# Linear attention in a fused kernel: token outputs from one head's 64 rows at a time, a one-step remainder, and half the transposes

## The chip, the cores and the metric

The kernel runs on one core of one Trainium2 chip. The metric is the device time in microseconds (us) of one execution. Three timed runs of the kernel before gave 1415.54, 1417.77 and 1420.30 us; their median, 1417.77 us, is the time before. The profile comes from one further execution.

## The reference

```python
kv  = einsum('bhsd,bhse->bhde', k, v)          # 8 batches, 8 heads, 576 tokens, 64 x 64 per head
out = einsum('bhsd,bhde->bhse', q, kv)
x   = out / sqrt(mean(out * out, -1) + 1e-6) * g_norm     # then as 4608 tokens x 512
xn, en = x / |x|, expert_emb / |expert_emb|               # 8 experts
logits = xn @ en.T / tau                                  # each token goes to its best expert
y   = gate * (relu(x @ w1[e]) @ w2[e])                    # e: the token's expert
h   = y @ w_in
result = (h * cos(h)) @ w_out
```

Everything is float32. The change touches the first two lines and the numerators of the logits; the experts and the last two matrices are computed as before.

## The kernel before

The program has three stages that follow one another: attention with the routing of the tokens, the experts (`layer1`, `layer2`), and the last layer (`step`, `out_product`). Only the first is touched.

It walks 36 tiles of 128 tokens. Nine tiles make a round over two batches: four tiles of 128 tokens of each batch, and as the ninth the last 64 tokens of both. For a tile `t` the loop at L869 issues in this order:

- `emit_out(t)` (L672): for each of four head pairs a matmul over all 128 rows. The left side holds two heads' transposed queries on 64 rows each, the right side is `kvb`, a 128 x 144 block: the two heads' 64 x 64 matrices on its diagonal, zeros beside them, and 16 columns for the two heads' products with the 8 expert vectors. The ninth tile of a round takes 64 tokens from each of two batches, so there each matmul fills 64 columns of the array, and two of them stand side by side. The result is the PSUM tile `po`, of which there are three.
- `emit_square(t)` and `emit_root(t-1)` on ScalarE; `emit_qT(t+2)` (L660): four transposes of queries into PSUM and a copy on ScalarE.
- what the table `due` (L845) names for this tile: `kv_pair`, the sum over tokens for two heads of a coming batch (four steps over 128 tokens each, and the remainder of 64 tokens as two steps on 32 rows); `"t"`, `kv_transpose`: four 128 x 128 transposes of `kvb`; `"z"`, `kv_logits`: four matmuls of 128 x 16 that make the 16 columns.
- the counting matmuls for the routing (L778, L779), in every third tile, which write to unused columns of `po`.
- `emit_x(t)` (L698) on VectorE: the norm's root, then two reads of `po` of the tile before, scaled (`z`, `xg`). After the `xg` of a tile its `po` is free for a later `emit_out`. Between these, `advance` takes steps of `place(g)`: three tiles at a time, VectorE picks the expert, GpSimd counts, and GpSimd scatters the rows to DRAM with three indirect DMAs.

Each engine works in the order of issue. GpSimd's queue holds, for each group of three tiles, the cast `pi`, three scatters (L789), and the product `w` of the next group (L757), for which VectorE waits in L761. The token loads of all batches go out through SP's queue, three batches ahead. In the second part of the stage ScalarE and VectorE also split weights for the experts (`split_piece`).

When a batch's sums are done (`kv_pair` with `hp == 3`), ScalarE copies the two diagonal blocks into `kvb` with two copies of 64 partitions. The zeros around them were set once, at the start, by GpSimd. A float32 matmul is recorded as two matmuls and two weight loads, so four of them are eight records; a transpose is recorded once.

Of the kernel before, what the change touches and what calls it, by code (L numbers as in the profile page):

```python
# [21 lines left out]
DM = H * D  # L22
# [3 lines left out]
NTILE = NT // 128  # L26
KVW = 128 + 2 * E
XZ = DM + E
# [8 lines left out]
def tile_kernel(ctx, tc, q, k, v, g_norm, emb, tau, w1, w2, w_in, w_out, out):  # L37
# [435 lines left out]
    if True:  # L473
# [18 lines left out]

        kr, vr = (kp.tile([128, H, 2, D], F32, name=nm, tag=nm, bufs=1) for nm in ("kr", "vr"))

# [95 lines left out]
        def prepare_experts():  # L590
            nc.scalar.activation(out=en, in_=embt, func=ACTF.Square, accum_out=es[:, 0:1])
            nc.vector.tensor_scalar(out=es[:, 1:2], in0=es[:, 0:1], scalar1=1e-30, scalar2=None, op0=ALU.max)
            nc.scalar.activation(out=es[:, 2:3], in_=es[:, 1:2], func=ACTF.Ln)
            nc.scalar.activation(out=es[:, 3:4], in_=es[:, 2:3], func=ACTF.Exp, scale=-0.5)
            for _ in rsqrt_steps(es[:, 3:4], es[:, 1:2], 0.0, 1.0, es[:, 3:4], es[:, 4:5]):
                pass
            nc.vector.tensor_tensor(out=es[:, 5:6], in0=es[:, 0:1], in1=es[:, 3:4], op=ALU.mult)
            nc.vector.scalar_tensor_tensor(
                out=es[:, 5:6], in0=es[:, 5:6], scalar=1e-6, in1=taub, op0=ALU.add, op1=ALU.mult
            )  # L600
            nc.vector.reciprocal(out=es[:, 6:7], in_=es[:, 5:6])
            nc.vector.tensor_scalar(out=en, in0=embt, scalar1=es[:, 6:7], scalar2=None, op0=ALU.mult)
            pe = ps_t.tile([128, 4, 128], F32, name="qTp", tag="qTp")
            for hp in range(4):
                nc.tensor.transpose(out=pe[:, hp, 0:E], in_=en[:, hp * 128:(hp + 1) * 128], identity=ident[0:E, 0:E])
            for i in range(2):
                r = slice(64 * i, 64 * i + 64)
                nc.vector.tensor_scalar(out=gz[r, :, i, :], in0=pe[r, :, 0:E], scalar1=g2[r], scalar2=None, op0=ALU.mult)

# [3 lines left out]
        def kv_pair(b, hp):  # L613
            if hp == 0:
                kvp_t[b] = ps_s.tile([128, 4, 128], F32, name="kvp", tag="kvp")
            p, dst = kvp_t[b], kvb[b % 3]
            rr = slice(32 * (b % 4), 32 * (b % 4) + 32)
# [12 lines left out]
        kvs_t = {}  # L630

        def kv_transpose(b):
            dst = kvb[b % 3]
            p = ps_s.tile([128, 4, 128], F32, name="kvp", tag="kvp")
            for hp in range(4):
                nc.tensor.transpose(out=p[:, hp, :], in_=dst[:, hp, 0:128], identity=ident)
            kvs_t[b] = tp.tile([128, 4, 128], F32, name="kvs", tag="kvs")
            nc.scalar.activation(out=kvs_t[b], in_=p, func=ACTF.Copy)

        def kv_logits(b):  # L640
            a = kvs_t.pop(b)
            p = ps_s.tile([128, 4, 128], F32, name="kvp", tag="kvp").rearrange("p c x -> p (c x)")
            for hp in range(4):
# [4 lines left out]
            nc.scalar.activation(  # L648
                out=kvb[b % 3][:, :, 128:KVW], in_=p[:, 0:8 * E].rearrange("p (c x) -> p c x", c=4), func=ACTF.Copy
            )  # L650
# [19 lines left out]
        ms_t, po_t = {}, {}  # L670

        def emit_out(t, po):  # L672
# [12 lines left out]
        def emit_square(t):  # L685
            sq = tp.tile([128, H, D], F32, name="sq", tag="sq")
            nc.scalar.activation(out=sq.rearrange("p (c n) d -> p c (n d)", c=4), in_=po_t[t][:, :, 0:128], func=ACTF.Square)
            ms_t[t] = sq
# [9 lines left out]
        def emit_x(t):  # L698
# [15 lines left out]
            advance(1)  # L714
            po = po_t.pop(t - 1)
            yb = y.rearrange("p (c n o) -> p c n o", c=4, o=1)
# [4 lines left out]
            nc.vector.tensor_tensor(  # L721
                out=z.rearrange("p (c n) x -> p c n x", c=4), in0=po[:, :, 128:KVW].rearrange("p c (n x) -> p c n x", n=2),
                in1=yb.to_broadcast([128, 4, 2, E]),
                op=ALU.mult,
            )
            advance(1)
            nc.vector.tensor_tensor(
                out=xg[g][:, i, 0:DM].rearrange("p (c n d) -> p c n d", c=4, n=2),
                in0=po[:, :, 0:128].rearrange("p c (n d) -> p c n d", n=2), in1=yb.to_broadcast([128, 4, 2, D]), op=ALU.mult,
            )  # L730
# [11 lines left out]
        def place(g):  # L742
# [32 lines left out]
            yield RANK  # L775
            c0 = KVW + g % 4 * E * n
            prv = cur["po"][:, 0, c0:c0 + E * n]
# [91 lines left out]
        for t in range(NTILE):  # L869
# [526 lines left out]
```

## Time and profile before

| | us |
|---|---|
| median of three runs | 1417.77 |
| the profiled execution | 1422.97 |
| its span, first to last instruction | 1421.4 |
| TensorE busy in the span | 1355.4 |
| VectorE busy | 1017.4 |
| ScalarE busy | 843.2 |
| GpSimd busy | 234.7 |
| first and last token-output matmul (start) | 25.9 and 140.8 |

The token outputs, `kv_pair`, transposes and logits all lie in the first tenth of the span; the rest belongs to the experts and the last layer. A chain of waits is read backwards from the last instruction: at each step it names what released the instruction, or the instruction before it on its engine, so the TensorE pieces in it are the spacing of starts, without the pipeline's tail. In groups of instructions the mean duration does include that tail.

### The profile page before, as it was taken

The page shows a single profiled execution, that of the slowest core. Times are in us where ns is not written, and L with a number is a line of the kernel's source. Part 1 is how long each engine was busy: PE and PEld are TensorE (multiplying, and loading weights), DVE is VectorE, ACT ScalarE, POOL GpSimd, SP SyncE. Part 2 cuts the span into 40 slices and gives each one's busy share as a digit, 9 for nine tenths or more (in the row PEclk, how much of TensorE's full clock was granted, in tenths as well). Part 3 has the DMA queues.
Part 4 walks back from the last instruction along what each step waited for, and adds up shares of the span by engine and source line. Part 5 has one row for each costly group of instructions (what it writes and reads, how often), then busy time and mean ns, then how long its engine had stood idle before and what let it go on. Part 6 is the DMA issues. An engine that isn't in the chain of part 4 may idle for free.

```text
span 1421.4 us, 26588 instructions
## 1 busy us (share of the span) xinstructions
PE 1355.4 (95%) x9545; PEld 1256.0 (88%) x9545; DVE 1017.4 (72%) x2179; ACT 843.2 (59%) x1647; POOL 234.7 (17%) x281
## 2 busy tenths in 40 slices
PE   8997799999999999998899999999999999999995
PEld 8886799899999999987789889889889889889894
DVE  1668688798888888566677677676776767777662
ACT  3668344464555454346676777677666767667662
POOL 0244442232422334100010010101001010010101
PEclk8999899999999999999999999999999999999998
DMA  9997386878987786385575655746656565655630
GB/s 293 337 336 217 123 216 173 263 237 236 232 246 226 203 247 169 90 279 192 170 236 178 216 193 171 249 159 212 210 186 210 183 215 182 211 188 185 206 105 32
DMA packets 210212, 291.74 MB, mean 205 GB/s; under 512 B 23468, under 2 KB 117200, under 8 KB 208856
## 3 DMA queue, kind: packets, MB, share of 16 engines
q1 hardware_dynamic: 191112, 243.25, 55.6%
q0 software_dynamic: 7296, 29.45, 6.5%
q10 hardware_dynamic: 11664, 17.26, 4.0%
q8 instruction: 78, 1.28, 0.4%
q14 instruction: 62, 0.51, 0.1%
HBM read 241.42 MB, written 48.47 MB: 204 GB/s over the span
## 4 chain that ended last, share of the span: by engine, by line
PE 81%; DVE 7%; DMA 4%; ACT 3%; issue 2%; POOL 0%; SPq 0%; ACTq 0%; DVEq 0%; POOLq 0%
PE o L1206 27%; PE p L1113 24%; PE hps L233 12%; PE y L250 12%; PE po L677 2%; PE kvp L621 1%; DMA raw<-in_moe_w 1%; PE xp L216 1%; DVE ring L141 1%; PE qTp L665 1%; PE kvp L624 1%; DMA ws<-wa 1%; DVE ring L344 1%; ACT ring L343 1%; DMA xr<-xs 0%
## 5 line engine op out<-in xcount | busy, mean ns | idle before, releaser
L1206 PE MATMUL o<-ring,g 128*128 128x512 f32 x1728 | 415.1, 395 | 2.3 <-ACT ring L343 1.6
L1206 PEld LDWEIGHTS o<-ring,g 128*128 128x128 f32 x1728 | 319.7, 188 | 75.5 <-issue 1.8
L233 PE MATMUL hps<-xT,ring 128*128 128x304 f32 x1536 | 244.6, 309 | 8.1 <-DVE xT L222 6.2
L250 PE MATMUL y<-h,ring 128*128 128x304 f32 x1536 | 238.1, 304 | 4.3 <-issue 2.7
L233 PEld LDWEIGHTS hps<-xT,ring 128*128 128x128 f32 x1536 | 222.5, 191 | 9.7 <-DVE xT L222 6.9
L250 PEld LDWEIGHTS y<-h,ring 128*128 128x128 f32 x1536 | 222.1, 189 | 5.8 <-issue 3.6
L1138 DVE TENSOR_TENSOR r<-u,h 128x512 f32<-128x512 f32 x144 | 99.7, 693 | 104.8 <-ACT u L1137 101.2
L1218 POOL DMA_INDIRECT out<-o_sb,perm_i x36 | 39.4, 1095 | 792.8 <-ACT o_sb L1217 621.1
L1094 ACT ACTIVATE u<-h 128x512 f32<-128x512 f32 x144 | 89.9, 624 | 96.8 <-DVE h L1129 95.8
L239 ACT ACTIVATE h<-hps 128x304 fp32r<-128x304 f32 x128 | 53.5, 418 | 116.8 <-PE hps L233 115.5
L1133 ACT ACTIVATE r<-u 128x512 f32<-128x512 f32 x144 | 89.8, 623 | 53.7 <-DVE u L1098 53.7
L1095 ACT ACTIVATE r<-h 128x512 f32<-128x512 f32 x144 | 89.8, 624 | 45.2 <-DVE g L1147 45.2
L1113 PEld LDWEIGHTS p<-ring,wb 128*128 128x128 f32 x840 | 106.3, 194 | 6.7 <-DVE h L1129 5.3
L1113 PE MATMUL p<-ring,wb 128*128 128x256 f32 x840 | 107.2, 288 | 4.4 <-DVE h L1129 4.4
L1113 PEld LDWEIGHTS p<-ring,wa 128*128 128x128 f32 x840 | 104.7, 191 | 5.7 <-DVE h L1129 2.9
L1113 PE MATMUL p<-ring,wa 128*128 128x256 f32 x840 | 106.1, 286 | 3.3 <-DVE h L1129 2.3
L1137 ACT ACTIVATE u<-r,half_pi 128x512 f32<-128x512 f32 x144 | 104.2, 724 | 4.7
L174 POOL TENSOR_TENSOR gx<-xr,g_bc 76x512 f32<-76x512 f32 x64 | 105.4, 1674 | 3.1 <-ACT gx L183 3.1
L1098 DVE SCALAR_TENSOR_TENSOR u<-r,u 128x512 f32<-128x512 f32 x144 | 95.7, 688 | 13.4 <-ACT r L1095 10.7
L141 DVE TENSOR_TENSOR ring<-raw,ring 128x1024 fp32r<-128x1024 f32 x72 | 92.3, 1283 | 11.7 <-ACT ring L140 11.0
L1147 DVE TENSOR_TENSOR g<-r,g 128x512 fp32r<-128x512 f32 x144 | 92.8, 686 | 0.2 <-ACT g L1143 0.2
L240 DVE SCALAR_TENSOR_TENSOR h<-hps,h 128x304 fp32r<-128x304 f32 x128 | 59.5, 465 | 36.5 <-ACT h L239 31.4
(219 smaller groups left out, 1908.9 us busy)
## 6 DMA issues: line engine op xcount, KB each, us to landing
wa<-ws SPq DMA_DIRECT2D x252, 256.0 KB
wb<-ws SPq DMA_DIRECT2D x252, 256.0 KB
raw<-in_moe_w SPq DMA_DIRECT2D x144, 256.0 KB
ws<-wa SPq DMA_DIRECT2D x56, 256.0 KB
xr<-xs POOLq DMA_DIRECT2D x16, 627.0 KB
yT<-yo SPq DMA_DIRECT2D x64, 152.0 KB
km<-in_k SPq DMA_DIRECT2D x8, 1024.0 KB
vm<-in_v SPq DMA_DIRECT2D x8, 1024.0 KB
```

The costliest lines, as they stand in the source:

```text
L141: nc.vector.tensor_tensor(out=w[:, 1], in0=raw, in1=w[:, 0].bitcast(F32), op=ALU.subtract)
L174: nc.gpsimd.tensor_tensor(out=gx[:, r].rearrange("p (h d) -> p h d", h=H), in0=t[:, r, 0:DM].rearrange("p (h d) -> p h d", h=H), in1=g_bc[ ...
L233: nc.tensor.matmul(out=p[:, 0:CH], lhsT=w[:, a, k * 128:(k + 1) * 128], rhs=c["xT"][b_][k], start=(n == 0), stop=(n == 11),)
L250: nc.tensor.matmul(out=c["y"][d][:, 0:CH], lhsT=w[:, a, 512 + d * 128:512 + (d + 1) * 128], rhs=h[b_], start=(f == 0 and i == 0), stop=(f ...
L1094: nc.scalar.activation(out=u, in_=p, func=ACTF.Copy, scale=1.0 / (2 * math.pi))
L1095: nc.scalar.activation(out=r, in_=p, func=ACTF.Copy, scale=1.0 / (2 * math.pi), bias=ROUND)
L1098: V.scalar_tensor_tensor(out=u, in0=r, scalar=-ROUND, in1=u, op0=ALU.add, op1=ALU.subtract)
L1113: nc.tensor.matmul(out=out, lhsT=w[:, wi, a, k * 128:(k + 1) * 128], rhs=x[xi][:, b_, k * 256:(k + 1) * 256], start=(n == 0), stop=(n == 5),)
L1137: nc.scalar.activation(out=u, in_=r, func=ACTF.Sin, scale=-2 * math.pi, bias=half_pi)
L1138: V.tensor_tensor(out=r, in0=u, in1=h, op=ALU.mult)
L1147: V.tensor_tensor(out=g_[1], in0=r, in1=g_[0].bitcast(F32), op=ALU.subtract)
L1206: nc.tensor.matmul(out=ob[b][t], lhsT=g_[a][:, t * 128:(t + 1) * 128], rhs=w[:, b_, m * 512:m * 512 + 512], start=(q_ == 0 and m == 0 and ...
```

## The change

`kvb` loses the zeros: it holds, for each pair, 64 rows of one head and 64 of the other, each with 64 + 8 columns (`KVW` = 72 instead of 144). A token output is now one matmul per head: 64 rows, 72 columns. The two heads of a pair use the upper and the lower half of the array's rows and write to two PSUM banks. `po` is [128, 2, 512] instead of [128, 4, 256], and its readers step through it by half and pair. ScalarE copies a batch's sums once, 128 partitions, into a new tile `kvc`; GpSimd copies that into `kvb`. The transposes read `kvc`, two heads' columns of two pairs at a time, so there are two of them; the logits are four matmuls of 64 rows to 64 partitions. The remainder of 64 tokens is loaded as 64 rows (runs of 256 bytes in DRAM instead of 512) into one of two tiles, and summed in one step. The zeroing of `kvb` at the start is gone.

```diff
-KVW = 128 + 2 * E
+KVW = D + E
         def load_rem(src, t, b):
-            r = slice(32 * (b % 4), 32 * (b % 4) + 32)
-            nc.sync.dma_start(out=t[r], in_=src[b, :, 512:576, :].rearrange("h (p r) d -> p h r d", r=2))
+            r = slice(64 * (b % 2), 64 * (b % 2) + 64)
+            nc.sync.dma_start(out=t[b // 2 % 2][r], in_=src[b, :, 512:576, :].rearrange("h p d -> p h d"))
-        gz = ca.tile([128, 4, 2, E], F32, name="gz")
+        gz = ca.tile([128, 2, 2, 2, E], F32, name="gz")
+        kvc = ca.tile([128, 4, D], F32, name="kvc")
-        for t in kvb:
-            nc.gpsimd.memset(t, 0.0)
...
-            for r in range(2):
-                for h, o in ho:
-                    nc.tensor.matmul(out=o, lhsT=kr[rr, h, r, :], rhs=vr[rr, h, r, :], start=False, stop=(r == 1))
+            for h, o in ho:
+                nc.tensor.matmul(
+                    out=o, lhsT=kr[b // 2 % 2][rr, h, :], rhs=vr[b // 2 % 2][rr, h, :], start=False, stop=True
+                )
             if hp == 3:
-                for n in range(2):
-                    r = slice(64 * n, 64 * n + 64)
-                    nc.scalar.activation(out=dst[r, :, n * D:(n + 1) * D], in_=p[r, :, 0:D], func=ACTF.Copy)
+                nc.scalar.activation(out=kvc, in_=p[:, :, 0:D], func=ACTF.Copy)
+                nc.gpsimd.tensor_copy(out=dst[:, :, 0:D], in_=kvc)
...
-            for hp in range(4):
-                nc.tensor.transpose(out=p[:, hp, :], in_=dst[:, hp, 0:128], identity=ident)
-            kvs_t[b] = tp.tile([128, 4, 128], F32, name="kvs", tag="kvs")
-            nc.scalar.activation(out=kvs_t[b], in_=p, func=ACTF.Copy)
+            for a in range(2):
+                nc.tensor.transpose(out=p[:, a, :], in_=kvc[:, 2 * a:2 * a + 2, :], identity=ident)
+            kvs_t[b] = tp.tile([128, 2, 128], F32, name="kvs", tag="kvs")
+            nc.scalar.activation(out=kvs_t[b], in_=p[:, 0:2], func=ACTF.Copy)
...
-            for hp in range(4):
-                nc.tensor.matmul(
-                    out=p[:, hp * 2 * E:(hp + 1) * 2 * E], lhsT=a[:, hp, :],
-                    rhs=gz[:, hp].rearrange("p n x -> p (n x)"), start=True, stop=True,
-                )
+            for i in range(2):
+                for n in range(2):
+                    nc.tensor.matmul(
+                        out=p[64 * n:64 * n + 64, i * 2 * E:(i + 1) * 2 * E], lhsT=a[:, i, 64 * n:64 * n + 64],
+                        rhs=gz[:, i, n].rearrange("p i x -> p (i x)"), start=True, stop=True,
+                    )
...
-                    nc.tensor.matmul(
-                        out=po[rows, hp, 0:KVW],
-                        lhsT=a[:, hp, rows],
-                        rhs=kvb[bb % 3][:, hp],
-                        start=True, stop=True,
-                    )
+                    for n in range(2):
+                        h_ = slice(64 * n, 64 * n + 64)
+                        nc.tensor.matmul(
+                            out=po[rows, n, hp * KVW:(hp + 1) * KVW],
+                            lhsT=a[h_, hp, rows],
+                            rhs=kvb[bb % 3][h_, hp],
+                            start=True, stop=True,
+                        )
...
-            po = ps_o.tile([128, 4, 256], F32, name="po", tag="po")
+            po = ps_o.tile([128, 2, 512], F32, name="po", tag="po")
```

The two places below are on TensorE and on GpSimd. On TensorE, tiles 6 to 8 of the first round, from the transposes of batch 2 to the split ninth tile; before:

```order
L636 MATMUL kvp<-ident,kvb_152 128x128 x3
L677 MATMUL po<-kvb_151,qT 128x144 [waits DVE_49]
L677 MATMUL po<-kvb_151,qT 128x144 x3
L665 MATMUL qTp<-ident,qa_604 128x128 [waits Activation_49]
L665 MATMUL qTp<-ident,qa_604 128x128 x3
L644 MATMUL kvp<-gz,kvs 128x16 [waits Activation_49]
L644 MATMUL kvp<-gz,kvs 128x16 x3
L778 MATMUL po<-ohc,upper 128x24 [waits Activation_49]
L779 MATMUL po<-exc,ones 128x24 [waits Pool_49]
L677 MATMUL po<-kvb_150,qT 64x144 [waits DVE_49]
```

And the same stretch of the changed kernel:

```order
L647 MATMUL kvp<-ident,kvc 128x128
L694 MATMUL po<-kvb_153,qT 128x72 [waits DVE_49]
L694 MATMUL po<-kvb_153,qT 128x72 x7
L677 MATMUL qTp<-ident,qa_605 128x128 [waits Activation_49]
L677 MATMUL qTp<-ident,qa_605 128x128 x3
L656 MATMUL kvp<-gz,kvs 64x16 [waits Activation_49]
L656 MATMUL kvp<-gz,kvs 64x16 x3
L794 MATMUL po<-ohc,upper 128x24 [waits Activation_49]
L795 MATMUL po<-exc,ones 128x24 [waits Pool_49]
L694 MATMUL po<-kvb_152,qT 64x72 [waits DVE_49]
L694 MATMUL po<-kvb_152,qT 64x72
L694 MATMUL po<-kvb_153,qT 64x72 x2
```

The sequence and the waits stay; four token outputs become eight of half the rows and half the columns, and the transposes before and after them are still of the whole array.

On GpSimd, from the first group's product `w` to the next one's (`kvb` is written here now; the scatters are the three `DMA` rows); of the changed kernel:

```order
L773 TENSOR_TENSOR w<-w,tie 128x24 [waits DVE_49]
L639 COPY kvb_154<-kvc 128x4x64 [waits Activation_49]
L784 COPY exc<-run 128x8
L786 TENSOR_TENSOR exc<-exc,ohc 128x8 [waits DVE_49,Pool_49]
L786 TENSOR_TENSOR exc<-exc,ohc 128x8 [waits Pool_49]
L787 TENSOR_TENSOR run<-exc,ohc 128x8 [waits Pool_49]
L749 COPY xg<-nums 128x3x8
L803 CAST pi<-pf 128x3 [waits DVE_49]
L805 DMA xs<-xg,pi 36864x528 [waits Pool_49]
L805 DMA xs<-xg,pi 36864x528 x2
L773 TENSOR_TENSOR w<-w,tie 128x24 [waits DVE_49]
```

The copy into `kvb` is the only new row; it stands behind `w`, ahead of the counts `exc`, and waits for ScalarE's copy. Between the scatters and the next `w` nothing was added.

## Rows read from the trace of the kernel before

**Rows 1.** The page: busy time, share of the span, instructions of each engine
```profile
PE 1355.4 (95%) x9545; PEld 1256.0 (88%) x9545; DVE 1017.4 (72%) x2179; ACT 843.2 (59%) x1647; POOL 234.7 (17%) x281
```
**Rows 2.** Windows: stretch, length, busy time by engine, granted clock, DMA share, GB/s
```profile
40.00:60.00 20.00, 19.61 (x272) 17.59 (x273) 12.74 (x53) 13.21 (x32) 5.63 (x16) 1.00 1.11 308
60.00:80.00 20.00, 17.91 (x203) 15.73 (x201) 12.84 (x55) 13.49 (x35) 8.64 (x20) 1.00 1.08 362
...
120.00:130.00 10.00, 7.58 (x59) 6.68 (x58) 9.50 (x30) 9.83 (x22) 3.17 (x4) 1.00 0.68 208
```
**Rows 3.** Chain of waits, 46 to 58 us: start, length, what, records
```profile
46.13 1.18 PE po L677 x8
47.31 0.44 PE qTp L665 x4
47.74 0.44 PE kvp L636 x4
48.18 0.98 PE po L677 x8
...
49.60 0.86 PE kvp L644 x8
...
50.91 1.13 PE po L677 x16
52.04 0.59 PE qTp L665 x4
52.63 0.61 PE kvp L621 x16
53.24 0.38 PE kvp L624 x8
```
**Rows 4.** Chain of waits, 66 to 80 us
```profile
74.75 2.14 issue
...
77.42 0.61 DVE xg L727
...
78.07 1.25 PE po L677 x8
```
**Rows 5.** Waits, 26 to 142 us: who for whom, us in total, times, longest
```profile
DVE mx L761 <- issue: 9.3, 4, 2.9
```
**Rows 6.** Timeline of weight loads alone, 90.9 to 91.6 us: start, length, what
```profile
91.06 0.30 PEld L778 LDWEIGHTS po<-ohc,upper 128*128 128x128 f32 x2 [0.16 <-ACT sq L687]
91.28 0.30 PEld L779 LDWEIGHTS po<-exc,ones 128*128 128x128 f32 x2
91.50 0.19 PEld L677 LDWEIGHTS po<-kvb,qT 128*128 128x128 f32 x1
```
**Rows 7.** Chain of waits, 11 to 26 us
```profile
13.46 1.05 PE kvp L621 x16
14.51 0.62 PE kvp L624 x8
...
24.76 0.80 PE kvp L644 x8
```
**Rows 8.** The tile kvb: shortest, median, longest in ns; first and last start
```profile
L628 ACT ACTIVATE kvb<-kvp x16: 361/378/379, 19.1 to 120.0; 64x256 f32<-64x256 f32 x16
L570 POOL MEMSET kvb<- x3: 577/577/577, 2.6 to 3.6; 128x576 f32 x3
```
**Rows 9.** Groups of instructions, 26 to 142 us: busy us, mean ns, idle before
```profile
L727 DVE TENSOR_TENSOR xg<-po,y 128x512 f32<-128x512 f32 x33 | 22.5, 681 | 0.2 <-issue 0.2
...
L638 ACT ACTIVATE kvs<-kvp 128x512 f32<-128x512 f32 x7 | 4.1, 589 | 0.0
L174 POOL TENSOR_TENSOR gx<-xr,g_bc 76x512 f32<-76x512 f32 x3 | 3.7, 1272 | 0.0
```
**Rows 10.** DMA, 47.2 to 50.8 us: packets, and q1's packets, MB, share
```profile
DMA packets 1792, 1.05 MB, mean 292 GB/s; under 512 B 1045, under 2 KB 1789, under 8 KB 1789
...
q1 hardware_dynamic: 1789, 1.02, 110.2%
```

More of the change, by code (lines that the diff above doesn't have):

```diff
@@ L491, in tile_kernel @@
         km, vm, qm, qr = {}, {}, {}, {}
-        kr, vr = (kp.tile([128, H, 2, D], F32, name=nm, tag=nm, bufs=1) for nm in ("kr", "vr"))
+        kr, vr = ([kp.tile([128, H, D], F32, name=f"{nm}{i}", tag=f"{nm}{i}", bufs=1) for i in range(2)] for nm in ("kr", "vr"))
         def load_main(src, store, p, nm, b):
@@ L601, in prepare_experts @@
             nc.vector.reciprocal(out=es[:, 6:7], in_=es[:, 5:6])
-            nc.vector.tensor_scalar(out=en, in0=embt, scalar1=es[:, 6:7], scalar2=None, op0=ALU.mult)
-            pe = ps_t.tile([128, 4, 128], F32, name="qTp", tag="qTp")
-            for hp in range(4):
-                nc.tensor.transpose(out=pe[:, hp, 0:E], in_=en[:, hp * 128:(hp + 1) * 128], identity=ident[0:E, 0:E])
+            for a in range(2):
+                nc.vector.tensor_scalar(
+                    out=en[:, a * 256:a * 256 + 256].rearrange("x (n i e) -> x n i e", n=2, i=2),
+                    in0=embt[:, a * 256:a * 256 + 256].rearrange("x (i n e) -> x n i e", i=2, n=2),
+                    scalar1=es[:, 6:7], scalar2=None, op0=ALU.mult,
+                )
+            pe = ps_t.tile([128, 4, 128], F32, name="qTp", tag="qTp")
+            for a in range(2):
+                for n in range(2):
+                    nc.tensor.transpose(
+                        out=pe[:, 2 * a + n, 0:E],
+                        in_=en[:, (2 * a + n) * 128:(2 * a + n + 1) * 128], identity=ident[0:E, 0:E],
+                    )
             for i in range(2):
                 r = slice(64 * i, 64 * i + 64)
-                nc.vector.tensor_scalar(out=gz[r, :, i, :], in0=pe[r, :, 0:E], scalar1=g2[r], scalar2=None, op0=ALU.mult)
+                nc.vector.tensor_scalar(
+                    out=gz[r, :, :, i, :], in0=pe[r, :, 0:E].rearrange("p (a n) x -> p a n x", a=2),
+                    scalar1=g2[r], scalar2=None, op0=ALU.mult,
+                )
         kvp_t = {}
@@ L634, in kv_transpose @@
             p = ps_s.tile([128, 4, 128], F32, name="kvp", tag="kvp")
-            for hp in range(4):
-                nc.tensor.transpose(out=p[:, hp, :], in_=dst[:, hp, 0:128], identity=ident)
-            kvs_t[b] = tp.tile([128, 4, 128], F32, name="kvs", tag="kvs")
-            nc.scalar.activation(out=kvs_t[b], in_=p, func=ACTF.Copy)
+            for a in range(2):
+                nc.tensor.transpose(out=p[:, a, :], in_=kvc[:, 2 * a:2 * a + 2, :], identity=ident)
+            kvs_t[b] = tp.tile([128, 2, 128], F32, name="kvs", tag="kvs")
+            nc.scalar.activation(out=kvs_t[b], in_=p[:, 0:2], func=ACTF.Copy)
         def kv_logits(b):
@@ L642, in kv_logits @@
             p = ps_s.tile([128, 4, 128], F32, name="kvp", tag="kvp").rearrange("p c x -> p (c x)")
-            for hp in range(4):
-                nc.tensor.matmul(
-                    out=p[:, hp * 2 * E:(hp + 1) * 2 * E], lhsT=a[:, hp, :],
-                    rhs=gz[:, hp].rearrange("p n x -> p (n x)"), start=True, stop=True,
-                )
+            for i in range(2):
[3 more added lines that the diff above has]
+                        rhs=gz[:, i, n].rearrange("p i x -> p (i x)"), start=True, stop=True,
+                    )
             nc.scalar.activation(
-                out=kvb[b % 3][:, :, 128:KVW], in_=p[:, 0:8 * E].rearrange("p (c x) -> p c x", c=4), func=ACTF.Copy
+                out=kvb[b % 3][:, :, D:KVW], in_=p[:, 0:4 * E].rearrange("p (c x) -> p c x", c=4), func=ACTF.Copy
             )
@@ L676, in emit_out @@
                 for rows, bb in ([(slice(0, 128), b)] if b is not None else [(slice(0, 64), 2 * j), (slice(64, 128), 2 * j + 1)]):
-                    nc.tensor.matmul(
-                        out=po[rows, hp, 0:KVW],
-                        lhsT=a[:, hp, rows],
-                        rhs=kvb[bb % 3][:, hp],
-                        start=True, stop=True,
-                    )
+                    for n in range(2):
+                        h_ = slice(64 * n, 64 * n + 64)
[4 more added lines that the diff above has]
+                            start=True, stop=True,
+                        )
             po_t[t] = po
@@ L727, in emit_x @@
             nc.vector.tensor_tensor(
[L728 to L729 removed]
+                out=xg[g][:, i, 0:DM].rearrange("p (c n d) -> p n c d", c=4, n=2),
+                in0=po[:, :, :, 0:D], in1=yb.to_broadcast([128, 2, 4, D]), op=ALU.mult,
             )
@@ L775, in place @@
             yield RANK
-            c0 = KVW + g % 4 * E * n
+            c0 = 4 * KVW + g % 4 * E * n
             prv = cur["po"][:, 0, c0:c0 + E * n]
```

14 lines of the change are left out of this document (8 added, 6 removed).

## Prediction, made before the changed kernel ran

> **What bounds the kernel now.** I read the busy times first: TensorE is busy for 95% of the span [rows 1]. The change touches only the attention stage, so what counts is that stage. In its middle TensorE is busy for 19.61 of 20 us and then for 17.91 of 20, at a granted clock of 1.00, which is 2.4 GHz; VectorE and ScalarE stand near 13 of 20 [rows 2]. The chain of waits says what TensorE waits for. Between 46 and 54 us every piece shown is TensorE [rows 3]. Between 66 and 80 us it is not: 2.14 us of "issue", then VectorE's `xg`, then a token output that had waited for it [rows 4]. The list of waits names the place: VectorE's L761, four waits, 9.3 us in all [rows 5]. It needs GpSimd's `w`, which stands behind three scatters. So there are two bounds side by side: the sum of TensorE's work, and, once in three tiles, a loop from the counting matmuls over VectorE, three scatters and `w` back to VectorE and a token output. From about 105 us on VectorE sets the pace (9.50 of 10 us busy [rows 2]), and TensorE's work is worth little there. I take two thirds of what TensorE gains or loses in the first 27 tiles as visible, by those rows: a bound in most tiles, not in each third one.
>
> **Part by part.** I count for a round of nine tiles, in TensorE time.
>
> *Token outputs.* Eight records of 128 x 144 take 0.98 us [rows 3], 122 ns each. Now there are 16 records, in two halves of the array. What limits one half is not the 72 columns but the weights: each record loads 128 columns of queries. Where the matmul is short (24 columns), loads start at 91.06, 91.28 and 91.50 with two in each step, so one load takes 110 ns [rows 6]. The Trainium skill, "TensorE: Matmul & The Clock Gate", section LDWEIGHTS, says that a load costs by its columns and not by its rows, 128 columns at 1.2 per ns, 107 ns by an estimate; the trace agrees (110 ns), and this rule speaks against the change: half a row block saves nothing in the load.
>
> Do the halves run side by side? No row shows two row halves. The nearest rows are the column halves: the split ninth tile has 16 records in 1.13 us, 0.15 of that the entry, so two records stand in 122 ns, loads included [rows 3]. The bounds: 8 pairs x 0.110 = 0.89 us, if row halves behave like column halves; 16 x 0.110 = 1.77 us, if loads go one after another. A lower end is 8 x 0.060 = 0.48 us, if nothing but the columns counted (72 of 144). I take 0.89, the row that it is nearest to: -0.09 per tile.
>
> *Changes of the array's division.* A step from the whole array to halves, or back, costs: the split tile 1.13 against 0.98, the transposes after it 0.59 against 0.44, so 0.15 each; after the 32-row remainder 1.18 against 0.98, 0.20 [rows 3]. Before, token outputs and transposes were both of the whole array. Now every tile pays 0.15 between them, and 0.15 at the next token output where no `kv_pair` stood between (there was a step there anyway). The Trainium skill, "TensorEngine Tiling (Array Packing)", section Key Properties, has it that a change of mode drains the engine; the trace agrees, with 0.15 us. Bounds: 0 to 0.30.
>
> *Remainder.* Eight records in 0.38 us, 16 of the main steps in 0.61: a pair is (0.61 - 0.38) / 4 = 0.058 us [rows 3]. Two pairs fewer: -0.115 per `kv_pair`.
>
> *Transposes, logits.* Two of four transposes go: -0.22 of 0.44. The logits' 0.86 us is eight whole loads; now four pairs of 64 columns, 0.23, with 0.15 to enter and 0.15 to leave.
>
> *Ninth tile.* 32 records in four quarters instead of 16 in two halves; loads of 64 columns, a round of four at a pair's 0.058: 0.46 for 0.98. -0.50.
>
> The sum for a round: four tiles with `kv_pair` 4 x (-0.09 + 0.15) = +0.24; their and the ninth tile's remainders 8 x -0.115 = -0.92; two tiles with transposes 2 x (-0.09 + 0.30 - 0.22) = -0.02; two with logits 2 x (-0.09 + 0.15 + 0.30 - 0.63), one of them with 0.15 more before the counting matmuls, = -0.39; the ninth -0.50. Together -1.6 us. Three rounds: -4.8, of which two thirds show: **-3.2 us**. The fourth round has no `kv_pair` and counts for nothing.
>
> *Start.* Four remainders at half clock: (1.05 - 0.62) / 4 = 0.108 per pair [rows 7], 4 x -0.215 = -0.86; I give half of it back, since the work that moves forward then runs at the low clock: -0.43. Logits 0.80 [rows 7] to 0.4 and two transposes: -0.6. **-1.0 us.**
>
> *ScalarE.* Two copies of 378 ns become one with as many elements per partition, so -0.38 eight times [rows 8]; the copy `kvs` goes from 512 to 256 elements, 589 to about 378 ns [rows 9]. Off the path mostly, since ScalarE idles a third of the time; where a transpose waits for `kvb`, twice or so: **-0.4 us.**
>
> *VectorE.* `xg` reads as many elements, 681 ns [rows 9], in runs of 64. At the memset's 1.0 ns per element [rows 8] some 170 of them are fixed; were they paid once for each half, +0.17 x 27 x 2/3 = +3.0; the other bound is 0, with nothing to gain in the same elements. I take **+0.3**, near 0, since it stays one instruction.
>
> *GpSimd.* 8 copies of 256 elements come, three memsets of 577 ns at the start go [rows 8]. By the memset's 1.0 ns per element and a two-input operation's 2.5 (1272 / 512 [rows 9]), a copy takes 0.26 to 0.64 us. What hides it: it is issued three tiles before the first token output that waits for it, and it is never put between the scatters and `w`. Queued behind it are the counts `exc`, for which the counting matmuls wait two tiles later. If this cover were gone, each copy would cost its 0.64 us, 5 us in all; I take 0.
>
> *DMA.* A remainder's runs are halved: 512 more packets per batch. In a stretch with 1045 small packets, 1789 took 110.2% of 16 engines over 3.6 us [rows 10], 35.5 ns each, so at most 512 x 35.5 / 16 = 1.1 us of queue per batch, at least 0. The chain holds no load between 26 and 100 us, so I take 0.
>
> Sum: -3.2 - 1.0 - 0.4 + 0.3 = -4.3, rounded to -4. Against the profiled execution (1422.97 us, 1.6 outside its span) that is 1419; the runs shown have a median of 1417.77, 5.2 lower, by the spread of executions alone, and a gain in the first tenth moves over whole. Forecast: **1413.8 us.**
>
> **Rivals.** *The row halves take turns (slower).* Then a token output takes 1.77 us, +0.88 a tile against the forecast's. For: the queries' loads are the limit and no row shows row halves side by side. Against: column halves do run so, loads included. 36 tiles take 115 us, six of them 20: +5.3 per 20, of which TensorE's idle 0.4 to 2.1 per 20 us absorb some, so about +4 per 20 over the 79 us to 105: +16; with the rest of the sum, -4, about **1430**. It decides as soon as a pair takes over 0.2 us.
>
> *The loads are not the limit (faster).* The Trainium skill, "TensorEngine Tiling (Array Packing)", section Theoretical Speedup, gives up to 2x for a contraction of 64 rows or fewer; nothing here shows it for row halves. In rows: a token output in 0.48 us, 0.41 less than forecast, x 27 x 2/3 = -7.4: **1406.4**. Against it stand the 110 ns.
>
> *Changing the division costs double (no gain).* Entry and exit at 0.30 instead of 0.15, about two a tile: +0.3 x 27 x 2/3 = +5.4: **1419.2**. For it: the 0.15 were seen with column halves only. The GpSimd copy gone from cover would give the same.
>
> **How the numbers follow.** A measurement of this kernel tells about 0.3% from no change, so the bounds are 1413.5 and 1422.0. Forecast 0.52 (its own range 1409.5 to 1418.5), turns 0.16, loads no limit 0.10, double 0.22. The forecast lies on the lower bound: half faster. Faster: 0.26 + 0.09 + 0.01 = 0.36. Slower: 0.16 + 0.07 of the doubled case + 0.01 = 0.24. The same: 0.40. The range 1407 to 1428 leaves out most of the two outer cases and holds about 0.8.
>
> **What would show it.** In the trace after: 16 token-output records in a chain piece of 0.9 to 1.1 us (1.8: turns; 0.6: no load limit); transposes after them 0.59; a remainder piece of 0.26; logits near 0.4; `mx` in VectorE still waiting for GpSimd about as long. The time of the experts' first matmul should come 4 us earlier. I am wrong if TensorE's work shrinks as counted and this start doesn't move: then the scatter loop holds more than a third of the stage. A granted clock under 1.00 between 26 and 130 us would also break the sum.

## The result, and the profile after

| kernel | median of its runs | ratio to before, 95% interval | profiled execution | its span |
|---|---|---|---|---|
| before | 1419.03 us (4 runs, the three of above and one more) | 1 | 1422.97 us | 1421.4 us |
| changed | 1438.2 us (4 runs, 1432.55 to 1443.12) | 1.0137 [1.0093, 1.0181] | 1436.94 us | 1435.3 us |

The change makes the kernel slower by 1.4%. The time lies above the predicted range.

The page of the changed kernel, busy time and the granted clock in 40 slices of the span:

```profile
PE 1373.9 (96%) x9721; PEld 1269.8 (88%) x9721; DVE 1017.6 (71%) x2180; ACT 840.2 (59%) x1639; POOL 237.3 (17%) x286
...
PEclk8765799999999999999899999999999999999998
```

Against [rows 1], TensorE is busy 18.5 us longer, though its work was to shrink. The second line says why: in the slices 2 to 5, some 36 to 179 us, the granted clock is 0.5 to 0.7 in the mean. The windows of the changed kernel, cut where the clock changes (columns as in [rows 2]: the last three numbers are the granted clock as a share of 2.4 GHz, the DMA share and GB/s):

```profile
20.00:30.00 10.00, 8.84 (x116) 7.87 (x114) 0.69 (x1) 3.10 (x6) 0.00 (x0) 0.97 1.18 267
31.00:54.00 23.00, 21.48 (x198) 18.03 (x200) 9.39 (x37) 11.48 (x27) 0.77 (x3) 0.50 1.11 276
55.00:85.00 30.00, 26.39 (x414) 22.33 (x410) 18.11 (x79) 20.22 (x52) 14.32 (x34) 1.00 1.07 310
86.00:136.00 50.00, 50.00 (x476) 42.92 (x476) 26.02 (x103) 24.73 (x58) 15.87 (x36) 0.50 0.81 236
...
154.00:170.00 16.00, 12.44 (x100) 11.18 (x101) 15.23 (x40) 8.26 (x19) 7.38 (x9) 0.50 0.64 164
```

Before, all of 40 to 130 us was at 1.00, 2.4 GHz: [rows 2], and these windows of the kernel before, the last of which is its only low one between 26 and 160 us:

```profile
80.00:100.00 20.00, 19.34 (x249) 16.96 (x249) 12.73 (x55) 12.52 (x32) 8.61 (x20) 1.00 1.10 344
100.00:120.00 20.00, 18.36 (x242) 15.81 (x241) 14.81 (x55) 14.85 (x35) 9.72 (x21) 1.00 0.76 249
...
142.00:150.00 8.00, 3.96 (x18) 3.73 (x17) 7.79 (x20) 2.87 (x8) 2.47 (x3) 0.50 0.25 77
```

Now there are three stretches at 0.50, 1.2 GHz; the last of them, at the end of the stage, has its counterpart before. From 86 to 136 us TensorE is busy for 50.00 of 50 us: there it alone is the bound, at half its speed. The other number to see is the last of the first line: the loads move 267 GB/s from 20 to 30 us. The kernel before moved in the same ten microseconds (its DMA, packets and rate):

```profile
DMA packets 4394, 3.35 MB, mean 335 GB/s; under 512 B 1134, under 2 KB 4393, under 8 KB 4393
```

Where the full clock is granted, the work shrank as counted. The timeline of TensorE in the changed kernel at 1.00 (start, length, engine, line, what, records, idle time before):

```profile
56.92 1.11 PE L694 MATMUL po<-kvb,qT 64*128 64x72 f32 x16
57.96 0.66 PE L677 MATMUL qTp<-ident,qa 128*128 128x128 f32 x4
58.55 0.41 PE L656 MATMUL kvp<-gz,kvs 128*64 128x16 f32 x8
58.89 0.40 PE L794 MATMUL po<-ohc,upper 128*128 128x24 f32 x2
...
59.45 0.73 PE L694 MATMUL po<-kvb,qT 64*64 64x72 f32 x32
...
61.79 0.33 PE L634 MATMUL kvp<-vr,kr 64*64 64x64 f32 x4
62.05 0.69 PE L632 MATMUL kvp<-vm,km 128*64 128x64 f32 x16
```

The time of a group is best read from start to next start. The 16 records of a token output take 57.96 - 56.92 = 1.04 us; the transposes behind them 0.59, the logits 0.34, the remainder 62.05 - 61.79 = 0.26. The same groups at 0.50, again the changed kernel:

```profile
99.89 1.12 PE L632 MATMUL kvp<-vm,km 128*64 128x64 f32 x16
100.94 0.48 PE L634 MATMUL kvp<-vr,kr 64*64 64x64 f32 x4
101.35 1.98 PE L694 MATMUL po<-kvb,qT 64*128 64x72 f32 x16
103.27 1.11 PE L677 MATMUL qTp<-ident,qa 128*128 128x128 f32 x4
```

Now a token output takes 103.27 - 101.35 = 1.92 us and the main steps 1.05 instead of 0.61 [rows 3]. At the low clock these groups take 1.7 to 1.85 times as long.

At the start, TensorE of the changed kernel:

```profile
28.36 1.11 PE L694 MATMUL po<-kvb,qT 64*128 64x72 f32 x16
32.22 1.11 PE L677 MATMUL qTp<-ident,qa 128*128 128x128 f32 x4 [2.74 <-ACT qT L679]
```

and the waits of the changed kernel from 26 to 142 us (us in total, times, longest):

```profile
...
DVE mx L777 <- POOL w L773: 14.5, 7, 3.3
...
ACT qa L586 <- DMA qm<-in_q: 4.6, 1, 4.6
```

ScalarE waits 4.6 us for a load of queries, TensorE stands idle behind it, and the clock is at 0.50 when it comes back (1.11 us for four transposes, which take 0.66 at full clock). So the first low stretch has a late load ahead of it. The second has none, but idle time of TensorE too, 1.93 us for VectorE's `xg`, in the timeline of the changed kernel:

```profile
85.85 1.98 PE L694 MATMUL po<-kvb,qT 64*128 64x72 f32 x16 [1.93 <-DVE xg L743]
```

The first expert matmul shows what the stage cost; before, and then changed:

```profile
146.46 7.33 PE L233 MATMUL hps<-xT,ring 128*128 128x304 f32 x36 [4.04 <-DVE xT L222]
```

```profile
166.03 7.43 PE L233 MATMUL hps<-xT,ring 128*128 128x304 f32 x36 [3.21 <-DVE xT L222]
```

It is 19.6 us late, as much as the 1.4% of the runs (0.0137 x 1419 = 19.4). In this one profiled execution 5.7 of them come back later, since the span is only 13.9 longer; where was not followed up.

### The profile page after: what moved, and what is told of

The parts are those of the page before. It is cut to its first block, busy times and chain, and to the rows that moved or that the text cites. A ratio compares the mean times of both kernels' runs of the same rounds, so it can differ in the third digit from the quotient of the medians.

```text
span 1435.3 us, 26940 instructions
## 1 busy us (share of the span) xinstructions
PE 1373.9 (96%) x9721; PEld 1269.8 (88%) x9721; DVE 1017.6 (71%) x2180; ACT 840.2 (59%) x1639; POOL 237.3 (17%) x286
```

## The experiments

Two theories, and a third beside them. *Clock*: the shorter records (72 columns for 144, fewer transposes and remainders) change what TensorE does, and the granted clock falls. *Load*: something in the loads starves TensorE at the start, and the clock falls for that. *Work*: the parts cost TensorE more than counted at any clock.

Two numbers serve for all: the ratio to the kernel before, run beside it on the same chip, and the mean granted clock from 20 us to the first expert matmul.

| kernel | ratio, 95% interval | first expert matmul, us | mean clock from 20 us to there |
|---|---|---|---|
| before | 1 | 146.5 | 0.97 |
| changed | 1.0137 [1.0093, 1.0181] | 166.0 | 0.70 |
| rem_only | 0.9986 [0.9969, 1.0002] | 144.3 | 0.97 |
| rem_only again | 1.0001 [0.9988, 1.0015] | | |
| no_rem | 1.0268 [1.0209, 1.0326] | 182.7 | 0.60 |
| no_halves | 1.0056 [1.0039, 1.0073] | 150.2 | 0.96 |
| wide | 1.0091 [1.0063, 1.0120] | 157.8 | 0.90 |
| after_pad | 1.0093 [1.0060, 1.0126] | 166.1 | 0.68 |
| before_shift | 1.0031 [1.0013, 1.0049] | 154.0 | 0.92 |
| no_rem_pad | 1.0228 [1.0189, 1.0267] | 165.4 | 0.70 |
| wide_pad | 0.9999 [0.9978, 1.0020] | 148.8 | 0.95 |
| wide_pad_act | 0.9995 [0.9983, 1.0007] | 150.6 | 0.94 |
| rem_fill | 1.0035 [1.0019, 1.0050] | 157.6 | 0.95 |

The last two columns are those of one profiled execution, the ratio that of all runs. Such an execution need not be a typical one: that of after_pad took 10.1 us more than the median of its runs, that of no_rem_pad 8.5 us less. But the mean granted clock of whole executions, which every run recorded, says the same as the table: 0.933 to 0.963 in all 19 runs of the four kernels with row halves of 72 columns (changed, no_rem, after_pad, no_rem_pad), 0.969 to 0.985 in every run of the others and of the kernel before.

**rem_only: the new remainder alone.**

```diff
-        kr, vr = (kp.tile([128, H, 2, D], ...) for nm in ("kr", "vr"))
+        kr, vr = ([kp.tile([128, H, D], ...) for i in range(2)] for nm in ("kr", "vr"))
...
-            for r in range(2):
-                for h, o in ho:
-                    nc.tensor.matmul(out=o, lhsT=kr[rr, h, r, :], rhs=vr[rr, h, r, :], start=False, stop=(r == 1))
+            for h, o in ho:
+                nc.tensor.matmul(out=o, lhsT=kr[b // 2 % 2][rr, h, :], rhs=vr[b // 2 % 2][rr, h, :], start=False, stop=True)
```

> The kernel before with only the new remainder: one step of 64 rows for each head, loaded in runs of 256 bytes. Clock theory (the token outputs in row halves and the shorter transposes and logits change what TensorE does, and the granted clock falls for that): the clock stays at 1.00 from 40 to 130 us and the time is that of before less some 0.115 us for each kv_pair, about 1416 to 1419 us. Rival 'load' (the short runs starve TensorE at the start, and the low clock follows from this): a stretch of 1.2 GHz in the attention stage and 1428 us or more. Rival 'work' (the parts cost TensorE time at any clock): about 1416 to 1419 here too, since this part only takes records away.

Measured: 0.9986 [0.9969, 1.0002], 1417.51 us. Its loads from 20 to 30 us:

```profile
DMA packets 4974, 3.41 MB, mean 341 GB/s; under 512 B 2150, under 2 KB 4974, under 8 KB 4974
```

Twice as many packets under 512 bytes as before, and no slower rate (341 against 335 GB/s). So the short runs do not slow the loads, and the remainder is not the culprit.

**no_rem: all but the remainder.** The diff is that of rem_only backwards, in the changed kernel.

> The changed kernel with the old remainder (two steps of 32 rows, runs of 512 bytes). Clock theory: the stretches of 1.2 GHz stay, 1430 to 1438 us. Rival 'load': the clock is 1.00 from 40 to 130 us and the time about 1415 us. Rival 'work': no stretch need go; about 1438 us, 0.5 us up or down for the remainders.

Measured: 1.0268, slower still than the changed kernel. The row of its windows from 20 us to the first expert matmul:

```profile
20.00:182.67 162.67, 151.23 (x1610) 130.21 (x1608) 84.57 (x301) 83.57 (x192) 46.02 (x99) 0.60 0.82 231
```

The low clock lasts longer (0.60 in the mean), and TensorE is busy for 151.23 of the 162.67 us. The measured 1457.64 us lie 20 us above the expected range, and why is not shown; that the short runs start the low clock is refuted from this side as well.

**no_halves: all but the row halves.**

```diff
-KVW = D + E
+KVW = 128 + 2 * E
...
-                            out=po[rows, n, hp * KVW:(hp + 1) * KVW], lhsT=a[h_, hp, rows], rhs=kvb[bb % 3][h_, hp],
+                            out=po[rows, hp, 0:KVW], lhsT=a[:, hp, rows], rhs=kvb[bb % 3][:, hp],
```

> The changed kernel with the token outputs as before: the whole array, 144 columns a record, a block diagonal of both heads; the new remainder, the two transposes and the copy on GpSimd stay. Clock theory: the clock is 1.00 from 40 to 130 us, 1414 to 1420 us. Rival 'load': low stretches stay, 1430 us or more. Rival 'work': what the row halves cost in divisions of the array goes (0.15 us a change, some 60 changes, so about 9 us): 1429 us with the clock as it was in the changed kernel.

Measured: 1.0056 [1.0039, 1.0073], 1426.29 us; windows from 20 us to the first expert matmul:

```profile
20.00:150.25 130.25, 103.16 (x1178) 88.70 (x1177) 83.46 (x301) 83.04 (x200) 51.53 (x108) 0.96 0.93 289
```

Most of the loss is gone with the row halves, and the long low stretches too; short ones are left (0.91 in the mean from 60 to 100 us). It stays 6 us above the expected 1414 to 1420. This kernel has a second GpSimd copy and a second copy of the logits into `kvb` for each batch, which the changed one has not, so the 0.6% isn't put down to one thing.

**wide: row halves, but 144 columns a record.** The loads, the record count and the divisions of the array stay.

```diff
-                            out=po[rows, n, hp * KVW:(hp + 1) * KVW], ... rhs=kvb[bb % 3][h_, hp],
+                            out=po[rows, n, hp * KVW:(hp + 2) * KVW], ... rhs=kvb[bb % 3][h_, hp:hp + 2].rearrange("p c x -> p (c x)"),
```

> The changed kernel, but each token-output record of a row half streams 144 columns instead of 72: its own head pair's block and the next one's, whose columns the next record writes again (the last pair's neighbour is a block of zeros). The same count of records, the same loads, the same divisions of the array and the same results. Clock theory: the granted clock stays 1.00 from 40 to 130 us and the time falls to 1414 to 1420 us, although TensorE streams twice the columns in the token outputs. Rival 'load': low stretches stay, 1436 us or more. Rival 'work': the same time or longer than the changed kernel, 1438 us or more, since no step is taken away.

Measured: 1.0091 [1.0063, 1.0120], 1432.29 us. The second stretch, from 86 to 136 us in the changed kernel, is gone up to 100 us, which the theory of the work can't explain; the window of wide from 40 to 100 us:

```profile
40.00:100.00 60.00, 53.77 (x805) 44.64 (x803) 39.18 (x161) 40.33 (x103) 23.34 (x54) 1.00 1.05 290
```

The clearest pair is the first stretch. In wide TensorE waits at the same place for as long as in the changed kernel (2.82 and 2.74 us), and the clock falls behind it too; but it is back at 40 us and not at 55. The timeline and a window of wide:

```profile
33.29 1.11 PE L679 MATMUL qTp<-ident,qa 128*128 128x128 f32 x4 [2.82 <-ACT qT L681]
```

```profile
33.00:40.00 7.00, 6.71 (x64) 5.63 (x65) 2.00 (x7) 2.50 (x7) 0.54 (x2) 0.52 1.10 266
```

So the columns do not keep the clock from falling; they go with how long it stays down, 7 us here and 24 in the changed kernel. But the kernel is not at 1414 to 1420 us, so something else costs too. Its loads from 20 to 30 us:

```profile
DMA packets 3993, 2.47 MB, mean 247 GB/s; under 512 B 2074, under 2 KB 3993, under 8 KB 3993
```

This was the clue. The kernels fall into two groups: 335, 341 and 327 GB/s in the kernel before, rem_only and no_halves, and 267, 298 and 247 in the changed one, no_rem and wide, with the same queue of transfers. It begins before TensorE does anything new: from 16 to 22 us, ahead of the first token output at 24 us, a packet of 1024 bytes took 49 to 51 ns in the mean in the second group and 46 to 47 in the first. What the two groups differ in is where the loads land. The program's own addresses follow from its tile sizes: `kvb` shrinks from three tiles of 2304 bytes per partition to three of 1152, `kvc` adds 1024, and `kvs` shrinks by 2 x 1024, together 4480 bytes. What is allotted behind them, `km`, `vm`, `qm`, `kr` and `vr` among it, moves down by that (`qr`, which lies ahead of `kvs`, by 2432 bytes), and so from a multiple of 512 to 128 bytes past one. In wide they stand 480 bytes past one; in the three quick kernels at a multiple. (The traces hold no addresses: this is counted from the tile sizes, with the tiles before the change taken to start at a multiple of 512.)

**after_pad, before_shift, no_rem_pad, wide_pad: only the addresses.** One unused tile behind the small attention tiles, 384, 128, 384 and 544 bytes.

```diff
+        ca.tile([128, 96], F32, name="pad")
         nc.scalar.dma_start(out=embt, in_=emb)
```

> The changed kernel with one unused tile of 384 bytes per partition behind the small attention tiles. By the tile sizes the change had moved everything behind them 4480 bytes down, so the loads of keys, values and queries land at 128 bytes past a multiple of 512; with the tile they land at a multiple of 512 again, as in the kernel before. No instruction changes. Theory 'address' (the loads' packets take longer at the moved addresses, 62 ns instead of 51 for 1024 bytes between 20 and 30 us, TensorE is starved at the start and the granted clock falls for it): packets back at 51 ns, no wait of 4.6 us for the queries, the clock at 0.95 or more in every stretch of 20 us from 40 to 120 us, and 1412 to 1421 us. Rival 'clock' (TensorE's own shorter work lowers the clock): the packets may be faster, but the stretches of 1.2 GHz stay and the time is 1430 to 1440 us.

> The kernel before with one unused tile of 128 bytes per partition behind the small attention tiles, so that the loads of keys, values and queries land 128 bytes past a multiple of 512. No instruction changes. Theory 'address': the 1024-byte packets take 58 to 64 ns instead of 51 between 20 and 30 us, TensorE waits for loads early in the stage, and the time rises by 5 to 25 us, more if the clock falls as well. Rival 'clock': 1417 to 1421 us, as before.

> The changed kernel with the old remainder (which took 1457.6 us), and the unused tile of 384 bytes. Theory 'address': the stretches of 1.2 GHz go and the time is 1414 to 1424 us, within 5 us of the changed kernel with that tile. Rival 'clock': 1445 us or more.

> The changed kernel with token-output records of 144 columns (which took 1432.3 us), and an unused tile of 544 bytes, which brings the loads back to multiples of 512. Theory 'address': 1412 to 1421 us, and no gain over the changed kernel with its unused tile. If both causes hold, this one is the fastest of the four, since it has neither the slow packets nor the shorter records. Rival 'clock' alone: about 1432 us, as without the tile.

Measured: the loads of after_pad from 20 to 30 us, and then those of before_shift:

```profile
DMA packets 4880, 3.32 MB, mean 332 GB/s; under 512 B 2149, under 2 KB 4880, under 8 KB 4880
```

```profile
DMA packets 3931, 2.89 MB, mean 289 GB/s; under 512 B 1105, under 2 KB 3931, under 8 KB 3931
```

No instruction is changed in either, and the rate follows the address both ways: 267 to 332 GB/s and 335 to 289. On the kernel before, the address alone costs 1.0031 [1.0013, 1.0049], 4.4 us where 5 to 25 were expected. The Trainium skill, "DMA: Bandwidth & Descriptors", section How a descriptor splits into AXI transactions, says that a descriptor is cut at multiples of 256 bytes, so that one of 256, 512 or 1024 bytes which starts elsewhere takes a transaction more; it speaks of reads. The trace agrees in kind for these writes: from 20 to 30 us the packets of 1024 bytes took 62 ns in the mean in the changed kernel and 51 in after_pad, those of 256 bytes 28 and 19; in before_shift and before it is 60 and 51, 23 and 18.

But after_pad is still at 1.0093, 1432.45 us, where 1412 to 1421 were expected if the address were all; its rival, that the low stretches stay, said 1430 to 1440. Its windows:

```profile
20.00:39.00 19.00, 16.98 (x222) 14.97 (x223) 5.50 (x18) 10.54 (x24) 0.54 (x2) 0.93 1.11 337
40.00:104.00 64.00, 64.00 (x604) 54.73 (x604) 29.77 (x122) 29.49 (x71) 17.65 (x43) 0.50 1.00 299
```

The first low stretch begins now at 40 instead of 31 us, and it lasts 64 us, with TensorE busy through all of it. What TensorE did ahead of it, in the timeline of after_pad:

```profile
38.78 0.69 PE L633 MATMUL kvp<-vm,km 128*64 128x64 f32 x16 [0.76 <-ACT kvb L661]
...
39.65 1.97 PE L695 MATMUL po<-kvb,qT 64*128 64x72 f32 x16
```

No load is waited for there; the idle time is 0.76 us, for ScalarE. The list of waits has one earlier wait for queries, after_pad from 20 to 41 us:

```profile
ACT qa L587 <- DMA qm<-in_q: 1.7, 1, 1.7
```

The kernel wide_pad differs from this one only in the 144 columns of a record and what goes with them: a block of zeros behind each `kvb`, and its pad. (That the block moves `kvc` was not tested apart.) Its windows, and its token output at 77 us:

```profile
20.00:40.00 20.00, 16.77 (x237) 14.34 (x237) 6.38 (x21) 10.55 (x24) 0.54 (x2) 1.00 1.11 327
40.00:78.00 38.00, 34.40 (x520) 28.74 (x518) 24.60 (x104) 24.22 (x61) 15.45 (x39) 1.00 1.06 331
78.00:85.00 7.00, 7.00 (x72) 5.59 (x70) 4.06 (x19) 3.84 (x10) 2.18 (x3) 0.51 1.08 360
85.00:139.00 54.00, 44.26 (x636) 36.55 (x632) 41.75 (x148) 38.97 (x90) 22.88 (x51) 1.00 0.86 269
```

```profile
77.29 1.59 PE L697 MATMUL po<-kvb,qT 64*128 64x144 f32 x16 [2.13 <-DVE xg L746]
```

The clock is at 1.00 for all but 7 of the 119 us, and the kernel is at 0.9999 [0.9978, 1.0020]. The one low stretch stands behind a wait of 2.13 us; TensorE is busy through all of it, as in the 64 us of after_pad, and here the clock is back after 7. Idle time isn't the difference: from 20 to 40 us wide_pad is the less busy of the two (16.77 of 20 us, against 16.98 of 19), and it waits longer for its queries, in its own list of waits from 20 to 41 us:

```profile
ACT qa L589 <- DMA qm<-in_q: 3.2, 1, 3.2
```

Its token output costs 71.64 - 70.46 = 1.18 us in its timeline, 0.14 more than with 72 columns:

```profile
70.46 1.25 PE L697 MATMUL po<-kvb,qT 64*128 64x144 f32 x16
71.64 0.66 PE L680 MATMUL qTp<-ident,qa 128*128 128x128 f32 x4
```

So there are two causes, and each is shown by a pair of kernels with intervals apart: the columns (after_pad against wide_pad, 1432.45 and 1421.86 us) and the address (wide against wide_pad, 1.0091 and 0.9999). Why records of 72 columns leave the clock low for longer, with TensorE busy all the while, no run shows, nor why one of after_pad's, from 128 to 135 us, is as short as those with 144. The two don't add up: against wide_pad each alone costs 0.9%, both 1.4%. (A TensorE at half speed asks less of the loads; that this is why was not tested.) Between the changed kernel and after_pad, 1.0137 and 1.0093, the intervals overlap. no_rem_pad, expected within 5 us of after_pad if the address were all, came out 17.4 us above it (1449.88): the address alone doesn't explain no_rem, and why its low stretches are so long stays open.

**before_shift256: 256 bytes past the multiple of 512 instead of 128.** The diff is that of before_shift with a tile of 256 bytes.

> The kernel before with the loads 256 bytes past a multiple of 512 instead of 128. If it is 256 bytes that count, the packets of 1024 bytes take 51 ns as in the kernel before between 20 and 30 us, and the time is 1417 to 1424 us; if it is 512 bytes, they take about 60 ns as with 128 bytes and the time is 1420 to 1430 us.

Measured in a single execution: 1421.4 us, and the loads from 20 to 30 us

```profile
DMA packets 4470, 3.43 MB, mean 343 GB/s; under 512 B 1132, under 2 KB 4469, under 8 KB 4469
```

A multiple of 256 is enough: 343 GB/s, and 50.5 ns in the mean for a packet of 1024 bytes.

**wide_pad_act: the copy into kvb on ScalarE.**

```diff
-                nc.gpsimd.tensor_copy(out=dst[:, 0:4, 0:D], in_=kvc)
+                nc.scalar.activation(out=dst[:, 0:4, 0:D], in_=p[:, :, 0:D], func=ACTF.Copy)
```

> The changed kernel with records of 144 columns and the unused tile (which took 1421.9 us), and the copy into kvb taken from GpSimd: ScalarE copies the key-value products from PSUM a second time instead. If the GpSimd copy stands in the path of counts, scatters and w (it was seen between w and exc, 0.41 us), the time falls by up to 8 x 0.4 = 3 us, to 1418 to 1420 us. If it was hidden, as the prediction had it, the time stays within 2 us of 1421.9, or rises by the 8 x 0.38 us of ScalarE.

Measured: 0.9995 [0.9983, 1.0007], against 0.9999 with GpSimd's copy. No difference, so the copy was hidden.

**rem_fill: idle time of TensorE filled at the end of the stage.**

```diff
+            if t >= 30:
+                fill(po, 10 if t == 34 else 5 if t < 34 else 0)
...
+        fill(cur["po"], 10)   # ahead of the first expert matmul
```

> The kernel before with the new remainder (1417.5 us), and 40 matmuls of 128 rows by 112 columns that compute nothing that is read, put where TensorE waits at the end of the stage: five behind the work of each of the tiles 30 to 33, ten behind tile 34 and ten ahead of the first expert matmul. Clock theory: the stretch of 1.2 GHz from 138 to 148 us goes or starts later, the first expert's matmuls run at 2.4 GHz, and the time falls by 1 to 4 us, to 1414 to 1416 us, though TensorE has 8 us of work more. If idle time of TensorE has nothing to do with that stretch, it stays and the time rises by 0 to 5 us.

Measured: 1.0035 [1.0019, 1.0050], a miss. TensorE in rem_fill:

```profile
153.34 4.58 PE L873 MATMUL po<-ones 128*128 128x112 f32 x20 [7.48 <-DVE xg L728]
```

The fall of the clock did move, from 138 us in rem_only to 149 here; a window of rem_only, and one of rem_fill:

```profile
139.00:148.00 9.00, 5.60 (x29) 4.99 (x26) 8.76 (x23) 3.65 (x9) 3.28 (x3) 0.50 0.21 62
```

```profile
120.00:149.00 29.00, 22.68 (x190) 20.32 (x188) 24.64 (x71) 21.56 (x47) 11.34 (x16) 1.00 0.68 183
```

But the last ten fillers write into a tile that VectorE still read, waited 7.48 us for it, and held up the experts to 157.6 us, where they began at 0.50 just the same. The experiment tests its own wait more than the theory; it says only that the stretch can be moved.

**rem_only again, with more rounds.**

> The kernel with the new remainder alone, taken again with more rounds, since it is the only version below the kernel before and its interval (0.9969 to 1.0002) reaches to no change. By the prediction's own terms the remainder is worth 24 x 0.115 x 2/3 = 1.8 us and 0.4 at the start, 2.2 us or a ratio of 0.9984; if that is right the interval stays under 1.0000. If the gain is only the scatter of executions, the ratio is 0.9995 to 1.0010.

Measured: 1.0001 [0.9988, 1.0015], 1417.9 us. The gain of the first runs isn't confirmed; the two intervals overlap, so a gain of 0.1% isn't ruled out either. No version here beats the kernel before.

## Why the prediction was wrong

**The step that failed** is the premise under every term of the sum: that the stage keeps its clock. The prediction took the 1.00 of [rows 2] as given, and named a lower one only in its last sentence, as what "would break the sum", with neither a chance nor a price. The price was to be had from the same rows. TensorE was busy for 19.61 and 17.91 of 20 us, the change took work from it, and [rows 7] show a group at half clock: 1.05 us for the main steps instead of the 0.61 of [rows 3]. By these two, 40 us at half clock hold what takes 23 us of TensorE's busy time at full clock, and at its busy share of 0.94 there (the mean of the two windows) 25 us of the span; so a rival "40 us of the stage at half clock" would have stood at +15 us, and decided alone. (The 40 us are picked with the result known; the changed kernel spent 73 us so between 31 and 136 us.) What the runs put in place of the premise: behind a wait of TensorE, 2.74 and 1.93 us in the changed kernel, 2.82 in wide and 2.13 in wide_pad, the clock fell with either width of record; with 72 columns it then stayed at 0.50 for 24 us and 50, with 144 for 7 and 7. In after_pad it was 64 us, behind waits of no more than 0.76 us.

**The DMA term** was sized at 0 to 1.1 us a batch from the count of packets, and set to 0. The count was indeed harmless (rem_only, 341 GB/s, and ratios of 0.9986 and 1.0001). What cost was the address of the loads, which stands in no line of the diff's text on loads: a smaller `kvb` moved them off a multiple of 256. It measures 0.3% on the kernel before and 0.9% on the wide one; on the changed kernel, 1.0137 against 1.0093, it is not clear of noise.

**The start**, forecast at -1.0 us, was in itself as good: the first token output begins at 24.3 us instead of 25.9. It was lost right behind, where the queries came 4.6 us late and TensorE stood idle for 2.74. The address is part of that at most: with it put right the wait for the queries was 1.7 us in after_pad, but 3.2 in wide_pad.

**The token outputs and changes of division** came out as forecast, at full clock: 0.89 + 0.15 was forecast, 1.04 measured. So row halves do run side by side, and both rivals that spoke of them fell: "the row halves take turns" (1.8 us; 16 x 0.110 is 1.76, not 1.77, which changes nothing) and "the loads are not the limit" (0.6). The doubled change of division fell with them: the transposes behind take 0.59, as forecast.

**Remainder, logits, ninth tile:** the remainder 0.26 (forecast 0.26), the logits 0.34 with their entry (forecast 0.38). The ninth tile's 32 records take 0.73 us with their tail (59.45 us above), where 0.46 and an entry of 0.15 were forecast; over three such tiles that is 0.4 us at most.

**ScalarE, VectorE and GpSimd:** groups of the changed kernel from 26 to 155 us (busy us, mean ns, idle before):

```profile
L743 DVE TENSOR_TENSOR xg<-po,y 128x512 f32<-128x512 f32 x31 | 21.1, 679 | 0.0
L639 POOL COPY kvb<-kvc 128x256 f32<-128x256 f32 x7 | 2.8, 400 | 30.0 <-ACT kvc L638 30.0
```

ScalarE's two copies, `kvc` and `kvs`, take 382 and 375 ns (forecast 378 for each). `xg` takes 679 instead of 681 ns, so the +0.3 was 0. GpSimd's copy takes 0.40 us, inside its bounds of 0.26 to 0.64, and is hidden (wide_pad_act).

**That two thirds of TensorE's gain show** was probably too much as well. With the clock nearly kept and the loads in place, wide_pad has the new remainder, transposes and logits, and TensorE is busy for 107.04 of its 128.84 us to the first expert matmul, against 109.34 of 126.46 before:

```profile
20.00:148.84 128.84, 107.04 (x1496) 89.06 (x1494) 83.61 (x301) 81.49 (x192) 46.17 (x99) 0.95 0.95 291
```

```profile
20.00:146.46 126.46, 109.34 (x1310) 96.55 (x1309) 84.14 (x301) 85.73 (x199) 42.81 (x91) 0.97 0.96 294
```

TensorE has 2.3 us less work and the experts begin 2.4 us later: what was saved, and more, is idle time of TensorE. The ratio alone doesn't settle it. By the forecast's terms wide_pad, with 0.14 us more in each token output, should gain 4.3 - 0.14 x 27 x 2/3 = 1.8 us, a ratio of 0.9987, which its interval of 0.9978 to 1.0020 holds; the remainder alone, worth 2.2 us (0.9984), measured 0.9986 once and 1.0001 [0.9988, 1.0015] the second time. `mx` still waits for GpSimd about as long, 14.5 us in the changed kernel; before it was 9.3 [rows 5] and, in three more waits that the prediction didn't count, 7.2. So that the loop over the scatters and `w`, named in the prediction, holds the stage fits the waits, but no run shortened it, and it is not shown.

## What to carry to other kernels

Before counting what TensorE saves, ask whether it keeps its clock with less to do, and give the case that it doesn't a chance and a price from rows at the low level. Ask what a shorter record is worth where its weight load stays: here half the columns saved 0.14 us a token output (1.18 to 1.04), and went with a clock that stayed low for 24 us and more at a time instead of 7. When a tile changes its size, look where the tiles behind it come to lie: a pad of 384 bytes was worth 65 GB/s from 20 to 30 us, and one of 544 bytes 0.9% of the wide kernel's time.

## What was not expected of the hardware

Loads into SBUF at 128 or 480 bytes past a multiple of 512 ran at 247 to 298 GB/s from 20 to 30 us (four kernels), those at multiples of 256 at 317 to 343 (nine), in the same queue and order of transfers. (The addresses are counted from tile sizes.)

Two row halves of the array work side by side with weight loads of 128 columns each: 16 records of 64 rows in 1.04 us, a change of division included.

After the same wait of 2.7 to 2.8 us the clock stayed at 0.50 for 24 us with records of 72 columns and for 7 us with records of 144, TensorE being busy for 21.48 of 23 us and 6.71 of 7 there.
